# Recurrence of the next chunk between the feed-forward matmuls of this one, two heads on the partitions

## The chip, the cores and the metric

The kernel runs on one core of a Trainium2 chip. The metric is device time in microseconds; three runs of the kernel before took 493.35, 493.57 and 493.63 us, median 493.57.

## What is computed

A gated linear recurrence over 768 steps for each of 4 x 8 heads of size 48, and a bilinear feed-forward on its output (3072 tokens of 384 features, 1536 hidden). The kernel computes the recurrence in chunks of 128 steps with cumulative products of alpha; products of matrices are in bf16, the cumulative sum of logarithms in fp32.

```python
for t in range(S):
    state = alpha[:, :, t, :, None] * state + np.einsum('bhd,bhe->bhde', k[:, :, t], v[:, :, t])
    y[:, :, t] = np.einsum('bhd,bhde->bhe', q[:, :, t], state)
x = np.ascontiguousarray(y.transpose(0, 2, 1, 3)).reshape(B * S, H * D)
a = x @ w_a
b = x @ w_b
out = (a * b) @ w_out
```

## The kernel before, in words

The work has two stages, one after the other.

The first is the recurrence, a loop over six chunks of 128 steps (L65). SP loads alpha, q, k and v of the chunk for all 32 heads, 768 KB each (L68 to L74), into tiles with two buffers. ACT takes the logarithm (L81); PE forms cumulative sums with a triangular fp32 matrix, 512 columns at a time (L89); ACT makes the exponentials beta and invb (L90, L91); DVE makes Qp, Kp and Vb (L94 to L98). Then comes a loop over the 32 heads (L102), in which every tile has 48 partitions or 48 columns: PE transposes Qp and Kp (L105, L109), DVE copies both out of PSUM (L107, L111), PE forms the scores (L114), DVE masks them (L116), PE adds two products into y (L119, L120), DVE copies y (L121), PE forms the state update (L124) and the chunk's decay (L126), ACT and DVE write the new state (L128 to L131). All PSUM tiles of this stage have one buffer. At the chunk's end SP writes y, transposed, to xT in memory (L136).

The second stage is the feed-forward. When the pools of the first are closed (L138), POOL issues the loads of the weights (L146 to L150) and SP reads xT back (L155). Six tiles of 512 tokens follow (L162): for each of 12 hidden blocks three matmuls with wa (L168), which ACT copies (L170), three with wb (L173), and a product on DVE (L174); then for each of four groups of 128 tokens 12 matmuls with wo (L178), a copy on ACT (L180) and a store (L181).

The order of instructions on each engine is set by a scheduler, which moves them within what the buffers allow; the weights wait for the pools of the first stage.

## Time and profile before

| what | value |
|---|---|
| median of three runs | 493.57 us |
| span of the profiled execution | 492.8 us |
| PE busy | 441.8 us (90%) |
| DVE busy | 256.5 us (52%) |
| ACT busy | 190.8 us (39%) |
| POOL busy | 11.2 us (2%) |
| moved by DMA | 32.32 MB |

The profile is of one execution, whose recorded time is the span from its first to its last instruction; it is 0.8 us shorter than the median of the runs. Busy times are shares of this span. PE is TensorE, PEld its weight loads, DVE VectorE, ACT ScalarE, POOL GpSimd and SP the engine that issues most transfers. Matmuls overlap on PE, so their busy times add up to more than the work takes one after the other.

### The profile page before, as it was taken

To read this page: it belongs to the slowest core of one execution; us is meant where nothing else is said; L and a number is where in the kernel's file an instruction comes from. 1 tells how busy PE (TensorE), PEld (TensorE's weight loads), DVE (VectorE), ACT (ScalarE), POOL (GpSimd) and SP (SyncE) were. 2 spreads that over 40 slices of the span, in tenths; PEclk is the share of its full clock that TensorE was granted. 3 is DMA by queue.
4 is the path that set the end of the run, shared out by engine and by line. 5 is a ranking of instruction groups with operands and counts; after the bars stand their busy time and mean duration, and the time that the engine had idled before them with its cause. 6 is when DMAs were issued, how large, how long until landed. Compare 5 with 4: busy or idle time off the path is not lost.

```text
span 492.8 us, 7155 instructions
## 1 busy us (share of the span) xinstructions
PE 441.8 (90%) x2280; PEld 225.2 (46%) x2292; DVE 256.5 (52%) x1052; ACT 190.8 (39%) x534; POOL 11.2 (2%) x28
## 2 busy tenths in 40 slices
PE   2589989999899989998999799942899999999997
...
GB/s 163 187 97 137 73 138 73 136 110 59 139 112 9 10 128 81 9 10 1 10 8 18 8 7 12 11 86 264 137 17 48 34 32 41 25 49 16 65 0 66
DMA packets 114806, 32.32 MB, mean 66 GB/s; under 512 B 109008, under 2 KB 113616, under 8 KB 114768
## 3 DMA queue, kind: packets, MB, share of 16 engines
...
q14 instruction: 20, 0.16, 0.1%
...
## 4 chain that ended last, share of the span: by engine, by line
PE 85%; DMA 5%; ACT 5%; DVE 2%; issue 2%; POOL 1%; ACTq 0%; POOLq 0%; DVEq 0%
PE bp L173 10%; PE op L178 9%; PE ap L168 9%; PE bl_p L126 9%; PE yt_p L120 9%; PE qpt_p L105 8%; PE qk_p L114 8%; PE kpt_p L109 8%; PE cumlog L89 8%; PE yt_p L119 5%; DMA wb_t<-in_moe_w_b_dram 3%; PE kv_p L124 3%; ACT logA L81 2%; DMA a_tile<-in_alpha_dram 1%; ACT invb L91 1%
## 5 line engine op out<-in xcount | busy, mean ns | idle before, releaser
L131 ACT ACTIVATE S_all<-tmp,bl 48x48 bf16<-48x48 f32 x192 | 63.6, 333 | 149.9 <-PE yt_p L120 144.1
L174 DVE TENSOR_TENSOR prod<-a_sb,bp 128x512 bf16<-128x512 bf16 x72 | 49.5, 688 | 105.9 <-PE bp L173 105.6
L121 DVE CAST yT_all<-yt_p 48x128 bf16<-48x128 f32 x192 | 54.3, 283 | 85.7 <-PE yt_p L120 85.3
L168 PE MATMUL ap<-xt_sb,wa_t 128*128 128x512 bf16 x206 | 59.6, 393 | 15.4 <-DMA wa_t<-in_moe_w_a_dram 12.8
L170 ACT ACTIVATE a_sb<-ap 128x512 bf16<-128x512 f32 x72 | 43.0, 597 | 69.6 <-PE ap L168 65.6
L126 PE MATMUL bl_p<-ones_col,logA 128*48 128x1 f32 x384 | 61.3, 229 | 5.4 <-ACT bl L128 4.8
L116 DVE TENSOR_TENSOR masked<-qk_p,mask_bf 128x128 bf16<-128x128 f32 x192 | 55.9, 291 | 14.7 <-PE qk_p L114 6.5
L126 PEld LDWEIGHTS bl_p<-ones_col,logA 128*48 128x48 f32 x384 | 45.6, 175 | 38.5 <-issue 10.5
L173 PE MATMUL bp<-xt_sb,wb_t 128*128 128x512 bf16 x214 | 60.6, 389 | 2.8 <-DMA wb_t<-in_moe_w_b_dram 2.5
L109 PE MATMUL kpt_p<-ident,Kp 128*48 128x128 bf16 x192 | 57.8, 301 | 2.9 <-DVE Kp L96 2.9
L105 PE MATMUL qpt_p<-ident,Qp 128*48 128x128 bf16 x192 | 57.4, 299 | 0.5 <-DVE Qp L94 0.4
L120 PE MATMUL yt_p<-QpT,S_all 48*48 48x128 bf16 x192 | 57.4, 299 | 0.0
L119 PE MATMUL yt_p<-masked,Vb 128*48 128x128 bf16 x192 | 53.7, 280 | 3.0 <-DVE Vb L98 1.0
L114 PE MATMUL qk_p<-QpT,KpT 48*128 48x128 bf16 x192 | 54.5, 284 | 0.2 <-DVE KpT L111 0.2
L89 PE MATMUL cumlog<-logA,ut_f 128*128 128x512 f32 x36 | 37.3, 1140 | 16.5 <-ACT logA L81 12.7
L178 PE MATMUL op<-wo_t,prod 128*128 128x384 bf16 x288 | 47.8, 326 | 0.0
L124 PE MATMUL kv_p<-Vb,Kp 128*48 128x48 bf16 x192 | 41.9, 218 | 0.6 <-DVE Vb L98 0.6
L111 DVE COPY KpT<-kpt_p 48x128 bf16<-48x128 bf16 x192 | 39.6, 206 | 0.3 <-PE kpt_p L109 0.3
L168 PEld LDWEIGHTS <-wa_t 128*128 128x128 bf16 x216 | 21.5, 100 | 40.0 <-issue 13.8
L107 DVE COPY QpT<-qpt_p 48x128 bf16<-48x128 bf16 x192 | 39.6, 206 | 0.0
L130 DVE TENSOR_TENSOR tmp<-kv_p,S_all 48x48 f32<-48x48 f32 x192 | 36.6, 190 | 2.0 <-PE qpt_p L105 1.4
L178 PEld LDWEIGHTS <-prod 128*128 128x128 bf16 x288 | 28.2, 98 | 19.3
...
## 6 DMA issues: line engine op xcount, KB each, us to landing
a_tile<-in_alpha_dram SPq DMA_DIRECT2D x6, 768.0 KB, 8.4
q_tile<-in_q_dram SPq DMA_DIRECT2D x6, 768.0 KB, 9.5
k_tile<-in_k_dram SPq DMA_DIRECT2D x6, 768.0 KB, 7.3
v_tile<-in_v_dram SPq DMA_DIRECT2D x6, 768.0 KB, 8.6
...
xT<-yT_all SPq DMA_DIRECT2D x24, 96.0 KB, 2.1
xt_sb<-xT SPq DMA_DIRECT2D x3, 768.0 KB, 6.8
...
```

Source lines behind the costliest of these rows:

```text
L89: nc.tensor.matmul(p[:, : ssl.stop - ssl.start], lhsT=ut_f32, rhs=logA[:, ssl], start=True, stop=True)
L105: nc.tensor.transpose(qpt_p, Qp[:, hd], ident)
L109: nc.tensor.transpose(kpt_p, Kp[:, hd], ident)
L114: nc.tensor.matmul(qk_p, lhsT=KpT, rhs=QpT, start=True, stop=True)
L119: nc.tensor.matmul(yt_p, lhsT=Vb[:, hd], rhs=masked, start=True, stop=False)
L120: nc.tensor.matmul(yt_p, lhsT=S_all[:, bh, :], rhs=QpT, start=False, stop=True)
L124: nc.tensor.matmul(kv_p, lhsT=Kp[:, hd], rhs=Vb[:, hd], start=True, stop=True)
L126: nc.tensor.matmul(bl_p, lhsT=logA[:, hd], rhs=ones_col, start=True, stop=True)
L131: nc.scalar.activation(out=S_all[:, bh, :], in_=tmp, func=AF.Copy, scale=bl)
L168: nc.tensor.matmul(ap, lhsT=wa_t[:, kk, ff * 128:(ff + 1) * 128], rhs=xt_sb[:, kk, rsl], start=(kk == 0), stop=(kk == KTILES - 1))
L173: nc.tensor.matmul(bp, lhsT=wb_t[:, kk, ff * 128:(ff + 1) * 128], rhs=xt_sb[:, kk, rsl], start=(kk == 0), stop=(kk == KTILES - 1))
L178: nc.tensor.matmul(op, lhsT=prod[:, ff, m * 128:(m + 1) * 128], rhs=wo_t[:, ff, :], start=(ff == 0), stop=(ff == NFF - 1))
```

## The change

Both stages are merged. Two heads stand side by side on the partitions, each in 64 rows of which 48 are used (Qp and Kp are zero-padded to 64 columns a head, Sb holds the states of a pair on its diagonal). One transpose, one y accumulation with Sb and one state update serve a pair; scores and the masked products are made for each head in its half of the partitions or output rows. Work goes by batch (8 heads): stA is the cumulative sum and the exponentials, stB the products Kp and Qp, now on POOL, and the cast of v, stC the transposes and one copy, stD scores and masks, stY y, stK the state update. y is copied by ACT into xT in SBUF; the 16 spare rows of each half are filled with features of the fourth pair by six small transfers (fill). The weights' rows are permuted in their loads to fit. The decay is the last row of beta, written to memory and read back with the other layout (decay).

The order is now written out by hand (manual_schedule: each engine gets its instructions as they are written). Chunk 0's recurrence is done first, batch by batch; then for each chunk c the 12 hidden blocks ff_a, ff_b of the feed-forward, with steps of the recurrence of chunk c+1 in slots (the table todo) between ff_a and ff_b, and the loads of chunk c+2 issued at block 0; then four ff_o. All loads of chunks 0 and 1 come first on SP. POOL issues the loads of the weights in pieces among its products of chunk 0.

```diff
-    for c in range(NCHUNK):
...
-        for bh in range(BH):
...
-            nc.sync.dma_start(out=xT_r[:, b, :, sl], in_=yT_r[:, b, :, :])
...
-        nc.sync.dma_start(out=xt_sb[:, kk, :], in_=xT[kk * 128:(kk + 1) * 128, :])
...
+    ctx.enter_context(tc.manual_schedule())
+    cst = ctx.enter_context(tc.tile_pool(name="cst", bufs=1))
+    ld = ctx.enter_context(tc.tile_pool(name="ld", bufs=2))
+    wk = ctx.enter_context(tc.tile_pool(name="wk", bufs=2))
+    dram = ctx.enter_context(tc.tile_pool(name="dram", bufs=2, space=bass.MemoryType.DRAM))
+    ps = ctx.enter_context(tc.tile_pool(name="ps", bufs=1, space=bass.MemoryType.PSUM))
...
+    def load_ab(i):
+        fs = slice(i * WS, (i + 1) * WS)
+        for w, t in ((moe_w_a, wa_t), (moe_w_b, wb_t)):
+            two = w[:KT * 2 * D, fs].rearrange("(t r d) f -> r d t f", r=2, d=D)
+            rest = w[KT * 2 * D:, fs].rearrange("(r t g) f -> r g t f", r=2, g=G)
+            for r in range(2):
+                nc.gpsimd.dma_start(out=t[r * DP:r * DP + D, :, fs], in_=two[r])
+                nc.gpsimd.dma_start(out=t[r * DP + D:(r + 1) * DP, :, fs], in_=rest[r])
+    def load_o(i):
+        n = NFF // 4
+        nc.gpsimd.dma_start(out=wo_t[:, i * n:(i + 1) * n, :],
+                            in_=moe_w_out[i * n * 128:(i + 1) * n * 128, :].rearrange("(k p) f -> p k f", p=128))
...
+    def alloc_loads(ch):
+        ch.a = ld.tile([C, B, H, D], F32, name="a_t")
...
+    def load(ch, b):
+        if b == 0:
+            alloc_loads(ch)
+        sl = slice(ch.c * C, (ch.c + 1) * C)
+        for t, src in ((ch.a, alpha), (ch.k, k), (ch.q, q), (ch.v, v)):
+            nc.sync.dma_start(out=t[:, b], in_=src[b, :, sl, :].rearrange("h s d -> s h d"))
...
+    def stA(ch, b):
+        p = ps.tile([C, 512], F32, name="t2")[:, :H * D]
+        nc.tensor.matmul(p, lhsT=ut_f32, rhs=ch.la[:, b], start=True, stop=True)
+        nc.scalar.activation(out=ch.beta[:, b], in_=p, func=AF.Exp)
+        nc.scalar.activation(out=ch.invb[:, b], in_=p, func=AF.Exp, scale=-1.0)
+    def stB(ch, b):
+        i = ch.c % 2
+        nc.gpsimd.tensor_mul(Kp[i][:, b, :, :D], ch.k[:, b], ch.invb[:, b].rearrange("p (h d) -> p h d", h=H))
+        nc.gpsimd.tensor_mul(Qp[i][:, b, :, :D], ch.q[:, b], ch.beta[:, b].rearrange("p (h d) -> p h d", h=H))
+        nc.vector.tensor_copy(ch.vb[:, b], ch.v[:, b])
+    def decay(ch):
+        if ch.c == NCH - 1:
+            return
+        row = dram.tile([1, B * P2, 2, D], F32, name="row")
+        nc.sync.dma_start(out=row.rearrange("o a r d -> o (a r d)"), in_=ch.beta[C - 1:C].rearrange("o b f -> o (b f)"))
+        for r in range(2):
+            nc.sync.dma_start(out=ch.bl[r * DP:r * DP + D].rearrange("d b a -> d (b a)"),
+                              in_=row[:, :, r, :].rearrange("o a d -> d (o a)"), allow_slow_non_contiguous=True)
+    def stC(ch, b):
+        i = ch.c % 2
+        t = ps.tile([C, 2, P2, C], BF16, name="t1")
+        for p in range(P2):
+            for j, src in enumerate((Qp[i], Kp[i])):
+                nc.tensor.transpose(t[:, j, p, :], src[:, b, 2 * p:2 * p + 2, :].rearrange("s h d -> s (h d)"), ident)
+        ch.qk = wk.tile([C, 2, P2, C], BF16, name="qk", bufs=3)
+        nc.vector.tensor_copy(ch.qk.rearrange("p j a s -> p (j a s)"), t.rearrange("p j a s -> p (j a s)"))
+    def stD(ch, b):
+        se = ps.tile([C, P2, C], F32, name="se")
+        so = ps.tile([C, P2, C], F32, name="so")
+        for p in range(P2):
+            nc.tensor.matmul(se[:, p, :], lhsT=ch.qk[0:DP, 1, p, :], rhs=ch.qk[0:DP, 0, p, :], start=True, stop=True)
+            nc.tensor.matmul(so[:, p, :], lhsT=ch.qk[DP:2 * DP, 1, p, :], rhs=ch.qk[DP:2 * DP, 0, p, :], start=True, stop=True)
+        ch.me = wk.tile([C, P2, C], BF16, name="me")
+        ch.mo = wk.tile([C, P2, C], BF16, name="mo")
+        nc.vector.tensor_mul(ch.me, se, mask4)
+        nc.vector.tensor_mul(ch.mo, so, mask4)
+        ch.qkD = ch.qk
+    def stY(ch, b):
+        y = ps.tile([C, P2, C], F32, name="t2")
+        for p in range(P2):
+            nc.tensor.matmul(y[:, p, :], lhsT=Sb[:, b, p, :], rhs=ch.qkD[:, 0, p, :], start=True, stop=False, skip_group_check=True)
+            nc.tensor.matmul(y[0:D, p, :], lhsT=ch.vb[:, b, 2 * p, :], rhs=ch.me[:, p, :], start=False, stop=True, skip_group_check=True)
+            nc.tensor.matmul(y[DP:DP + D, p, :], lhsT=ch.vb[:, b, 2 * p + 1, :], rhs=ch.mo[:, p, :], start=False, stop=True, skip_group_check=True)
+        nc.scalar.activation(out=ch.xT[:, :, b, :], in_=y[:, :KT, :], func=AF.Copy)
+        nc.scalar.activation(out=ch.y3[:, b, :], in_=y[:, KT, :], func=AF.Copy)
+    def fill(ch):
+        for r in range(2):
+            for t in range(KT):
+                nc.sync.dma_start(out=ch.xT[r * DP + D:(r + 1) * DP, t], in_=ch.y3[r * DP + t * G:r * DP + (t + 1) * G])
+    def stK(ch, b):
+        if ch.c == NCH - 1:
+            return
+        i = ch.c % 2
+        kv = ps.tile([C, 512], F32, name="t1")[:, :P2 * 2 * D].rearrange("p (a e) -> p a e", a=P2)
+        for p in range(P2):
+            nc.tensor.matmul(kv[:, p, :], lhsT=Kp[i][:, b, 2 * p:2 * p + 2, :].rearrange("s h d -> s (h d)"),
+                             rhs=ch.vb[:, b, 2 * p:2 * p + 2, :].rearrange("s h d -> s (h d)"), start=True, stop=True)
+        tmp = wk.tile([C, P2, D], F32, name="tmp")
+        for r in range(2):
+            rs = slice(r * DP, r * DP + D)
+            nc.vector.tensor_add(tmp[rs], kv[rs, :, r * D:(r + 1) * D], Sb[rs, b, :, r * DP:r * DP + D])
+            nc.gpsimd.tensor_mul(Sb[rs, b, :, r * DP:r * DP + D], tmp[rs],
+                                 ch.bl[rs, b, :].rearrange("p (a o) -> p a o", o=1).broadcast_to([D, P2, D]))
+    def ff_a(ch, f):
+        if f == 0:
+            ch.prod = wk.tile([128, NFF, NT], BF16, name="prod")
+        x = ch.xT.rearrange("p k b s -> p k (b s)")
+        ap = ps.tile([128, NT], F32, name="f", bufs=4)
+        for kk in range(KT):
+            nc.tensor.matmul(ap, lhsT=wa_t[:, kk, f * 128:(f + 1) * 128], rhs=x[:, kk, :], start=(kk == 0), stop=(kk == KT - 1))
+        ch.as_ = wk.tile([128, NT], BF16, name="as_", bufs=3)
+        nc.scalar.activation(out=ch.as_, in_=ap, func=AF.Copy)
+    def ff_b(ch, f):
+        x = ch.xT.rearrange("p k b s -> p k (b s)")
+        bp = ps.tile([128, NT], F32, name="f", bufs=4)
+        for kk in range(KT):
+            nc.tensor.matmul(bp, lhsT=wb_t[:, kk, f * 128:(f + 1) * 128], rhs=x[:, kk, :], start=(kk == 0), stop=(kk == KT - 1))
+        nc.vector.tensor_mul(ch.prod[:, f, :], ch.as_, bp)
+    def ff_o(ch, m):
+        op = ps.tile([128, NT], F32, name="f", bufs=4)[:, :d_model]
+        for f in range(NFF):
+            nc.tensor.matmul(op, lhsT=ch.prod[:, f, m * C:(m + 1) * C], rhs=wo_t[:, f, :], start=(f == 0), stop=(f == NFF - 1))
+        ot = wk.tile([128, d_model], F32, name="ot", bufs=3)
+        nc.scalar.activation(out=ot, in_=op, func=AF.Copy)
+        nc.sync.dma_start(out=out[m * S + ch.c * C:m * S + (ch.c + 1) * C, :], in_=ot)
+    for b in range(B):
+        load(chunks[0], b)
+    for b in range(B):
+        load(chunks[1], b)
+    c0 = chunks[0]
+    for b in range(B):
+        logs(c0, b)
+        stA(c0, b)
+        stB(c0, b)
+        if b == B - 1:
+            decay(c0)
+        if b == 1:
+            load_ab(0)
+        if b == 2:
+            load_ab(1)
+        stC(c0, b)
+        stD(c0, b)
+        stY(c0, b)
+    fill(c0)
+    for b in range(B):
+        stK(c0, b)
+    load_ab(2)
+    load_ab(3)
+    for i in range(4):
+        load_o(i)
+    logs(chunks[1])
+    stA(chunks[1], 0)
+    stB(chunks[1], 0)
+    stA(chunks[1], 1)
+    stB(chunks[1], 1)
+    for c in range(NCH):
+        ch = chunks[c]
+        nx = chunks[c + 1] if c + 1 < NCH else None
+        n2 = chunks[c + 2] if c + 2 < NCH else None
+        todo = {}
+        if nx is not None:
+            todo = {
+                0: lambda: stA(nx, 2), 1: lambda: stB(nx, 2), 2: lambda: (stC(nx, 0), stA(nx, 3)),
+                3: lambda: (stD(nx, 0), stB(nx, 3), decay(nx)), 4: lambda: stC(nx, 1), 5: lambda: (stY(nx, 0), stK(nx, 0), stD(nx, 1)),
+                6: lambda: stC(nx, 2), 7: lambda: (stY(nx, 1), stK(nx, 1), stD(nx, 2)), 8: lambda: stC(nx, 3),
+                9: lambda: (stY(nx, 2), stK(nx, 2), stD(nx, 3)), 11: lambda: (stY(nx, 3), fill(nx), stK(nx, 3)),
+            }
+        for f in range(NFF):
+            ff_a(ch, f)
+            if n2 is not None and f == 0:
+                for b in range(B):
+                    load(n2, b)
+            if n2 is not None and f == NFF - 1:
+                logs(n2)
+            if f in todo:
+                todo[f]()
+            ff_b(ch, f)
+        for m in range(B):
+            ff_o(ch, m)
+            if n2 is not None and m >= 2:
+                stA(n2, m - 2)
+                stB(n2, m - 2)
```

On PE, in the recurrence of before, one head of the loop stands in a row (names: yt_p is y, qpt_p and kpt_p are transposes, qk_p scores, bl_p decay, kv_p the state update):

```order
L119 LDWEIGHTS Vb
L119 MATMUL yt_p<-masked,Vb 48x128
L120 LDWEIGHTS S_all
L120 MATMUL yt_p<-QpT,S_all 48x128
L105 LDWEIGHTS Qp
L105 MATMUL qpt_p<-ident,Qp 48x128
L114 LDWEIGHTS KpT
L114 MATMUL qk_p<-QpT,KpT 128x128
L109 LDWEIGHTS Kp
L109 MATMUL kpt_p<-ident,Kp 48x128
L126 MATMUL bl_p<-ones_col,logA 48x1
```

On PE after the change, at slot 5 of chunk 0, the last of three matmuls of ff_a (f is the feed-forward's PSUM tile) is followed by the first pair of stY (t_582 is y; me and mo are the masked scores of the even and the odd head):

```order
L205 MATMUL f<-xT,wa_t 128x512
L171 LDWEIGHTS Sb
L171 MATMUL t_582<-qk,Sb 128x128
L172 LDWEIGHTS vb
L172 MATMUL t_582<-me,vb 48x128
L173 LDWEIGHTS vb
L173 MATMUL t_582<-mo,vb 48x128
```

The y matmuls, which stood among those of other steps of a head, now stand pair by pair between two groups of feed-forward matmuls.

On DVE, in the recurrence of before, one head reads:

```order
L121 CAST yT_all<-yt_p 48x128
L130 TENSOR_TENSOR tmp<-kv_p,S_all 48x48
L116 TENSOR_TENSOR masked<-qk_p,mask_bf 128x128
L107 COPY QpT<-qpt_p 48x128
L111 COPY KpT<-kpt_p 48x128
```

On DVE after the change, at slots 5 and 6 of chunk 0 (prod is the feed-forward's product, tmp the state sum, qk the copied transposes):

```order
L214 TENSOR_TENSOR prod<-as__558,f 128x512
L194 TENSOR_TENSOR tmp<-t_597,Sb 48x192 x2
L164 TENSOR_TENSOR me<-se,mask 128x512
L165 TENSOR_TENSOR mo<-so,mask 128x512
L214 TENSOR_TENSOR prod<-as__580,f 128x512
L154 COPY qk<-t_632 128x1024
```

Steps of the recurrence now stand, in larger tiles, between the feed-forward's products.

On POOL, which before only issued the weights' loads, the last weight loads now stand ahead of the products of chunk 1:

```order
L80 DMA wb_t<-in_moe_w_b_dram 48x3x384
L81 DMA wb_t<-in_moe_w_b_dram 16x3x384
L85 DMA wo_t<-in_moe_w_out_dram 128x3x384 x4
L133 TENSOR_TENSOR Kp_94<-k_t,invb 128x8x48
L134 TENSOR_TENSOR Qp_92<-q_t,beta 128x8x48
```

The products moved from DVE to POOL, behind the transfers that POOL issues.

## Rows read from the trace of the kernel before

**Rows 1.** Page, busy time by engine: us (share of the span) x instructions

```profile
PE 441.8 (90%) x2280; PEld 225.2 (46%) x2292; DVE 256.5 (52%) x1052; ACT 190.8 (39%) x534; POOL 11.2 (2%) x28
```

**Rows 2.** Stages: start:end length, busy of each engine (instructions), clock, DMA share, GB/s

```profile
67.50:119.28 51.78, 49.52 (x264) 25.72 (x263) 34.26 (x164) 22.69 (x74) 0.00 (x0) 1.00 0.69 102
326.70:349.57 22.87, 5.57 (x12) 1.31 (x14) 0.56 (x1) 0.87 (x3) 8.04 (x15) 1.00 0.95 229
349.57:353.40 3.83, 3.83 (x10) 1.36 (x9) 1.35 (x3) 1.01 (x2) 1.62 (x4) 1.00 1.27 190
353.68:489.15 135.47, 134.88 (x688) 68.17 (x697) 47.45 (x69) 52.48 (x92) 0.00 (x0) 1.00 0.10 34
489.15:492.80 3.65, 0.00 (x0) 0.00 (x0) 0.00 (x0) 0.49 (x1) 0.00 (x0) 1.00 0.16 57
```

**Rows 3.** Chain that ended last, in order of time: start us, us, what

```profile
8.55 2.06 PE cumlog L89 x2
...
349.77 1.71 PE ap L168 x4
...
354.28 0.65 PE ap L168 x3
...
364.64 7.80 PE op L178 x48
...
387.98 7.80 PE op L178 x48
```

**Rows 4.** Timeline, recurrence, PE: start us, us, engine line operation, idle before

```profile
24.30 0.30 PE L109 MATMUL kpt_p<-ident,Kp 128*48 128x128 bf16 x1
...
24.39 0.31 PE L105 MATMUL qpt_p<-ident,Qp 128*48 128x128 bf16 x1
...
100.86 0.30 PE L120 MATMUL yt_p<-QpT,S_all 48*48 48x128 bf16 x1
...
101.09 0.30 PE L105 MATMUL qpt_p<-ident,Qp 128*48 128x128 bf16 x1
...
101.19 0.28 DVE L121 CAST yT_all<-yt_p 48x128 bf16<-48x128 f32 x1 [0.36 <-PE yt_p L120]
```

**Rows 5.** Groups by line and shape: xcount | busy us, mean ns | idle before, releasers

```profile
L174 DVE TENSOR_TENSOR prod<-a_sb,bp 128x512 bf16<-128x512 bf16 x72 | 49.5, 688 | 105.9 <-PE bp L173 105.6 <-ACT a_sb L170 0.3
L170 ACT ACTIVATE a_sb<-ap 128x512 bf16<-128x512 f32 x72 | 43.0, 597 | 69.6 <-PE ap L168 65.6 <-PE bp L173 3.5
L107 DVE COPY QpT<-qpt_p 48x128 bf16<-48x128 bf16 x192 | 39.6, 206 | 0.0
L130 DVE TENSOR_TENSOR tmp<-kv_p,S_all 48x48 f32<-48x48 f32 x192 | 36.6, 190 | 2.0 <-PE qpt_p L105 1.4 <-ACT bl L128 0.2
L180 ACT ACTIVATE sb<-op 128x384 f32<-128x384 f32 x24 | 11.8, 491 | 38.6 <-PE op L178 38.6
L96 DVE TENSOR_TENSOR Kp<-k_tile,invb 128x1536 bf16<-128x1536 f32 x6 | 10.5, 1742 | 0.0
L81 ACT ACTIVATE logA<-a_tile 128x1536 f32<-128x1536 f32 x6 | 8.9, 1483 | 5.0 <-DMA a_tile<-in_alpha_dram 4.9
L81 ACT ACT_TABLE_LOAD x6 | 7.7, 1283 | 0.8 <-PEq L196 0.7
L98 DVE CAST Vb<-v_tile 128x1536 bf16<-128x1536 f32 x6 | 5.7, 949 | 0.0
```

**Rows 6.** POOL: a group by line, then its timeline at the weights' loads

```profile
masks.py:66 POOL TENSOR_SCALAR_AFFINE_SELECT ut_f<-ut_f 128x128 f32<-128x128 f32 x1 | 0.3, 283 | 0.0
...
332.64 1.12 POOL L150 DMA_DIRECT2D wo_t<-in_moe_w_out_dram  x2
338.55 0.53 POOL L150 DMA_DIRECT2D wo_t<-in_moe_w_out_dram  x1 [4.79 <-DMA wa_t<-in_moe_w_a_dram]
```

**Rows 7.** Page, DMA issues: out<-in xcount, KB each, median us to landing; and GB/s by slices

```profile
GB/s 163 187 97 137 73 138 73 136 110 59 139 112 9 10 128 81 9 10 1 10 8 18 8 7 12 11 86 264 137 17 48 34 32 41 25 49 16 65 0 66
...
a_tile<-in_alpha_dram SPq DMA_DIRECT2D x6, 768.0 KB, 8.4
xT<-yT_all SPq DMA_DIRECT2D x24, 96.0 KB, 2.1
```

More of the change, by code (lines that the diff above doesn't have):

```diff
@@ L12 @@
 AF = mybir.ActivationFunctionType
+ALU = mybir.AluOpType
 @with_exitstack
@@ L50 @@
     make_upper_triangular(nc, ut_f32, val=1.0, diag=True)
-    mask_bf = cst.tile([C, C], BF16, name="mask_bf")
-    make_upper_triangular(nc, mask_bf, val=1.0, diag=True)
-    ones_col = cst.tile([C, 1], F32, name="ones_col")
-    nc.vector.memset(ones_col, 1.0)
-    S_all = cst.tile([D, BH, D], BF16, name="S_all")
-    nc.vector.memset(S_all, 0.0)
-    gla = ExitStack()
-    chpool = gla.enter_context(tc.tile_pool(name="chunk", bufs=2))
-    hpool = gla.enter_context(tc.tile_pool(name="head", bufs=4))
@@ L138 @@
-    gla.close()
-    wpool = ctx.enter_context(tc.tile_pool(name="wpool", bufs=1))
-    KTILES = d_model // 128
-    NFF = d_ff // 128
-    wa_t = wpool.tile([128, KTILES, d_ff], BF16, name="wa_t")
-    wb_t = wpool.tile([128, KTILES, d_ff], BF16, name="wb_t")
-    for kk in range(KTILES):
-        nc.gpsimd.dma_start(out=wa_t[:, kk, :], in_=moe_w_a[kk * 128:(kk + 1) * 128, :])
-        nc.gpsimd.dma_start(out=wb_t[:, kk, :], in_=moe_w_b[kk * 128:(kk + 1) * 128, :])
-    wo_t = wpool.tile([128, NFF, d_model], BF16, name="wo_t")
@@ new lines @@
+    mask = cst.tile([C, C], BF16, name="mask")
+    make_upper_triangular(nc, mask, val=1.0, diag=True)
+    mask4 = mask.rearrange("p (o s) -> p o s", o=1).broadcast_to([C, P2, C])
+    Sb = cst.tile([C, B, P2, 2 * DP], BF16, name="Sb")
+    nc.vector.memset(Sb, 0.0)
+    Qp, Kp = [], []
+    for i in range(2):
+        t = cst.tile([C, B, H, DP], BF16, name=f"Qp{i}")
+        nc.vector.memset(t, 0.0)
+        Qp.append(t)
+        t = cst.tile([C, B, H, DP], BF16, name=f"Kp{i}")
+        nc.vector.memset(t, 0.0)
+        Kp.append(t)
@@ new lines, in load_o @@
+    def load_o(i):
+        n = NFF // 4
+        nc.gpsimd.dma_start(out=wo_t[:, i * n:(i + 1) * n, :],
+                            in_=moe_w_out[i * n * 128:(i + 1) * n * 128, :].rearrange("(k p) f -> p k f", p=128))
+    class Chunk:
+        pass
+    chunks = []
+    for c in range(NCH):
+        ch = Chunk()
+        ch.c = c
+        chunks.append(ch)
+    def alloc_loads(ch):
+        ch.a = ld.tile([C, B, H, D], F32, name="a_t")
+        ch.k = ld.tile([C, B, H, D], F32, name="k_t")
+        ch.q = ld.tile([C, B, H, D], F32, name="q_t")
+        ch.v = ld.tile([C, B, H, D], F32, name="v_t")
@@ new lines @@
+    logs(chunks[1])
[3 more added lines that the diff above has]
+    stB(chunks[1], 1)
+    for c in range(NCH):
+        ch = chunks[c]
[24 more added lines that the diff above has]
+                stB(n2, m - 2)
```

124 lines of the change are left out of this document (24 added, 100 removed).

## The prediction

> **What bounds the kernel now.** I read the page's busy shares first: PE is busy for 90% of the span, DVE for 52%, POOL for 2% [rows 1]. A busy PE alone says little, since its matmuls overlap, so I cut the span into stages [rows 2]. One chunk of the recurrence lasts 51.78 us with PE busy for 49.52 of it; six chunks fill the first 327 us. Then 22.87 us pass in which PE works for 5.57 us: x goes to memory and back and the weights arrive. The six feed-forward tiles take the last 139 us, and 3.65 us pass after the last matmul.
>
> The chain of waits shows what one feed-forward tile costs [rows 3]: its 48 output matmuls take 7.80 us, and those of the next tile begin 387.98 - 364.64 = 23.34 us later. It also shows the clock. Three 512-column matmuls take 0.65 us from 354.28 us on (0.216 us each, 512 columns at 2.4 GHz), but four take 1.71 us at 349.77 us (0.427 each, 512 at 1.2 GHz). The granted clock is printed as 1.00 for both stretches [rows 2]; the spacing decides, and by it PE ran at the lower level when the dense feed-forward began and rose within its first tile. For the recurrence the timeline agrees [rows 4]: two 128-column matmuls of one shape start 24.39 - 24.30 = 0.09 us apart, near 128 columns at 1.2 GHz (0.107), and pairs of different shapes 0.23 us apart (100.86 to 101.09). So the recurrence is a stream of small matmuls at the lower level, each paying about twice its columns. The feed-forward is at its columns already.
>
> **What the change does, part by part.** I write the new time as P + 5K + F + ends: a prologue P up to the first feed-forward matmul, five chunks K in which feed-forward c and recurrence c+1 share PE, one feed-forward tile F alone.
>
> *Removed:* the 22.87 us hand-over through memory, and the 192 x 8 small matmuls of the per-head loop (two of the eight are L126's one-column fp32 passes).
>
> *K, PE.* Feed-forward per chunk is what it was: 23.3 us at the upper level. Recurrence per batch is 8 transposes, 8 scores, 12 for y, 4 for the state: 32 matmuls, 128 per chunk for 32 heads. No 128-column matmul at the upper level is in the trace. Lower bound: the 384-column matmuls, 7.80/48 = 0.1625 us, a third of which is 0.054; upper bound: the 0.23 us of mixed shapes. Of the two I build a value: every matmul pays 0.054, and each change of shape the difference of the two rows at the lower level, 0.23 - 0.09 = 0.14. The changes per batch are two for each of the four pairs in y (full width, then 48 columns) and two around the scores, ten in all: 32 x 0.054 + 10 x 0.14 = 3.1 us, four times 12.5, nearer the lower bound, since most neighbours now have one shape. Bounds for the 128: 6.9 and 29.4. The cumulative sum is fp32: 2.06 us for 512 columns at the lower level [rows 3], so 1.55 for 384; at the upper level between half (0.8) and all of it; I take 1.0, four of them 4.0 us, bounds 3.2 and 6.2. PE together: 23.3 + 12.5 + 4.0 = 39.8.
>
> *K, the others* [rows 5], per chunk. DVE: 12 prod x 0.69, 8 masks x 0.69 (the same shape), 4 copies of 1024 (between 0.67 and 1.13 from the 0.206 of 128, I take 1.13), 8 state sums x 0.34, 4 casts x 0.3 = 22.2 us. ACT: 12 x 0.60, 12 x 0.49 (outputs and x), 8 exps x 0.49, 4 x 0.27, a log of 1.48 and two table loads of 1.28 = 20.2. POOL below 12. None reaches 39, so PE bounds the chunk if each slot's answer is back before the next slot. Between two slots lie one ff_b and one ff_a, 1.3 us, plus the slot's own matmuls; the longest answer, copy 1.13 behind a prod of 0.69, needs 1.8. I cost the handovers at 3 us a chunk, bounds 0 and 6. That cover is gone if DVE has a backlog. **K = 43**, bounds 33.4 and 65.
>
> One wait is new: the decay goes through memory (row, then two reads), queued on SP behind 16 loads of chunk c+2. Four loads of 768 KB, 8.4 us each to landing but overlapping, moved at some 170 GB/s, take about 18 us; add two transfers of 2.1 us [rows 7] and two lots of 768 four-byte pieces: the decay lands some 25 us after the chunk's start. The state product on POOL waits for it, and DVE's third state sum (slot 9, some 24 us in) waits for POOL because tmp has two buffers; behind it stand masks and prod. That is the handover I expect to see, 0 to 3 us, inside the 3 us above.
>
> *P.* It is a serial chain at the lower clock, four passes, one per batch, since each engine's order is fixed; durations are scaled from [rows 3 to 5]: log 0.49, sum 1.6, two exps 0.87, K and Q products on POOL, 8 transposes 1.06 (0.107 each and 0.2 to end), copy 1.13, scores 1.3 (8 x 0.16), masks 1.38, y 1.8 (the ten matmuls behind the masks, 0.16 each and 0.2), evictions 0.76, table load 1.28, and 0.6 for hand-overs. POOL has never multiplied here; its affine select of 128 columns took 0.283 us [rows 6], so 384 cost 0.85; the DVE product row (1.74 for 1536) would give 0.44. I take POOL's own row, 1.7 for two. Sum 14.0, four times 56, plus 3.5 until the first slice of alpha lands (between the 2.1 and the 8.4 us of [rows 7]), less one table load: 58. Then the four state updates and two cumulative sums of chunk 1, 9 us. **P = 67**, bounds 54 and 78. The casts of v on DVE run at the same time, and no row of before shows both engines at work on SBUF. The Trainium skill (SBUF — State Buffer, Who interferes with whom) says that DVE in a two-port copy or cast and GpSimd exclude each other for a whole instruction, which speaks against products on POOL; by it each product could wait for one cast of about 0.3 us, 1.2 us in the four passes, and the sum would be 316.
>
> *Chunk 0* pays extra, S. POOL issues 16 + 4 weight transfers before the products of chunk 1; an issue takes 0.55 us, and the ninth waited 4.79 us for the first to land [rows 6]. So the products come about 11 to 16 us after the state update, while slot 2 asks for them 8 us after the first matmul: a stall near 5 us, and some matmuls before and after it at the lower level, 4 us. **S = 9**, bounds 0 and 20. The last recurrence chunk has no state update and two sums less: -3. The ends are F = 23.3 and 3.7.
>
> Sum: 67 + 5 x 43 + 9 - 3 + 27 = **315 us**, against the 492.8 us span of the profiled execution; the median of the runs, 493.57, is 0.8 longer, which is nothing at this size. 0.2%, or 1 us, is about what a measurement of this kernel can tell from no change. With all bounds together it would be 245 or 447; terms that err independently give 280 to 350.
>
> **Rivals.** *Clock falls in the slots.* The rows that speak for it: the recurrence matmuls kept PE at the lower level for 327 us although PE was 90% busy. If the slots do so again and only ff_o runs fast, with 0.17 a small matmul (halfway between 0.107 and 0.23), a chunk is 72 x 0.427 + 7.8 + 128 x 0.17 + 2 x 1.6 + 2 x 1.0 = 65.5, and the time, with S = 0, 418. Against: dense feed-forward stands between all slots, and it raised the clock within one tile. *Handovers show.* If each of 11 slots waits 1.5 us for DVE (a copy and a hand-over) in place of 3 us in all, K = 56.5 and the time 382; for it speaks that DVE waited 0.36 us for PE in every head of before [rows 4], against it the 1.8 us reckoned above. *Heads run side by side.* Scores and masked products of a pair use different halves of the partitions or of the output rows. If they overlap on PE, the price falls to the lower bound 0.054 and, with no waits, K to 33.4, P to 60, S to 4, and the time is 255; no row speaks for it, since all heads of before use the same partitions, and against it stand the 0.23 us between neighbours of different rows [rows 4]. The Trainium skill (TensorE: Matmul & The Clock Gate, Part 3: Packing small matmuls) says that matmuls on different row or column groups run concurrently, about 4 ns apart; no run here shows it yet, and it is this rival. *Slower.* The clock stays low in the feed-forward as well, because slots interrupt it, and small matmuls cost what mixed shapes cost now, 0.23: F = 72 x 0.427 + 48 x 0.325 = 46.3, K = 46.3 + 29.4 + 4 x 1.6 = 82, P = 78, S = 0, the time 535. At 0.17 and P = 67 it would be 486; from 0.18 us a matmul on, with the clock always low, the change loses. There the change moves work under a matmul stream that became twice as long, so it would not do what it says.
>
> **How the numbers follow.** Forecast 0.52 (280 to 350), clock in the slots 0.17, handovers 0.16, side by side 0.10, slower or even 0.05. The range 275 to 410 holds the forecast, the handovers and the better half of the clock rival, 8 in 10. All but the last case are far faster: faster 0.95, within 0.2% 0.01, slower 0.04.
>
> **What would show it.** Right: ff_b and ff_a of three matmuls 0.65 us apart between slots; a chunk period of 38 to 48 us between two ff_o; 60 to 75 us before the first feed-forward matmul; POOL's products of chunk 1 late in slot 2. Wrong: 512-column matmuls 0.43 us apart in the slots of chunks 1 to 4 (clock); PE idle before me, mo or the copied qk in most slots (handovers); transposes or scores 0.2 us apart (price of a matmul); a period over 50 us.

## The result and the profile after

The changed kernel takes 281.94 us (median of four runs, 280.39 to 282.33) against 493.6 us: a ratio of 0.5705, 95% interval 0.5689 to 0.572. That is inside the predicted range and 2 us above the lower end of the forecast's own range (280 to 350); the value of 315 was 33 us too high. The profiled execution has a span of 280.6 us, 1.3 us below the median.

The page's busy times after the change (us, share of the span, instructions), to be read beside [rows 1]:

```profile
PE 231.5 (82%) x1520; PEld 120.6 (43%) x1520; DVE 120.3 (43%) x213; ACT 122.8 (44%) x219; POOL 89.7 (32%) x134
```

DVE has a fifth of its instructions left and less than half of its time; POOL now multiplies. The stages answer to [rows 2] (start:end length, busy of PE, PEld, DVE, ACT, POOL with counts, granted clock, DMA share, GB/s). They are cut at the first feed-forward matmul of each chunk; chunks 2 and 3 repeat chunk 1:

```profile
0.00:60.83 60.83, 26.37 (x141) 12.72 (x141) 17.48 (x31) 23.40 (x33) 24.75 (x46) 1.00 0.75 133
60.83:109.56 48.73, 40.01 (x258) 20.58 (x257) 19.17 (x36) 19.07 (x35) 22.22 (x34) 0.89 0.70 119
109.56:146.24 36.68, 36.03 (x257) 19.25 (x256) 19.60 (x36) 18.97 (x35) 11.84 (x17) 1.00 0.53 111
...
219.62:253.41 33.79, 33.48 (x238) 17.84 (x237) 16.62 (x26) 13.78 (x29) 7.17 (x8) 1.00 0.07 26
253.41:276.60 23.19, 23.19 (x121) 11.65 (x119) 8.24 (x12) 9.12 (x16) 0.00 (x0) 1.00 0.09 32
276.60:280.55 3.95, 0.31 (x2) 0.00 (x0) 0.00 (x0) 0.49 (x1) 0.00 (x0) 1.00 0.20 76
```

The 1.00 printed for the prologue is not what PE ran at: the clock record begins at 63.4 us only, and in the prologue the transposes of batch 1 start 0.107 us apart (six steps from 21.84 to 22.48 us), which is 128 columns at the lower level. From chunk 1 on PE is busy for 36.0 of 36.7 us, so it bounds the chunk, as predicted; DVE and ACT have half of it, POOL a third. Put into the prediction's sum:

| term | predicted | measured | difference in the sum |
|---|---|---|---|
| P, up to the first feed-forward matmul | 67 | 60.8 | -6.2 |
| K, one chunk, five times | 43 | 36.7 | -31.5 |
| S, extra of chunk 0 (48.73 - 36.69) | 9 | 12.0 | +3.0 |
| last recurrence chunk (33.79 - 36.69) | -3 | -2.9 | +0.1 |
| F and end | 27 | 27.1 | +0.1 |
| sum | 315 | 280.6 | -34.5 |

Inside a chunk, PE's timeline shows what a slot costs (start us, duration us, engine, line, operation; durations overlap, so spacings are read). It answers to [rows 4]; slots 6 and 7 of chunk 1:

```profile
127.49 0.81 PE L205 MATMUL f<-xT,wa_t 128*128 128x512 bf16 x3
128.14 0.22 PE L152 MATMUL t<-ident,Qp 128*128 128x128 bf16 x1
128.19 0.22 PE L152 MATMUL t<-ident,Kp 128*128 128x128 bf16 x1
...
129.23 0.81 PE L205 MATMUL f<-xT,wa_t 128*128 128x512 bf16 x3
129.88 0.22 PE L171 MATMUL t<-qk,Sb 128*128 128x128 bf16 x1
130.03 0.24 PE L172 MATMUL t<-me,vb 128*48 128x128 bf16 x1
130.03 0.24 PE L173 MATMUL t<-mo,vb 128*48 128x128 bf16 x1
130.20 0.23 PE L171 MATMUL t<-qk,Sb 128*128 128x128 bf16 x1
...
131.19 0.34 PE L189 MATMUL t<-vb,Kp 128*128 128x96 bf16 x4
131.47 0.23 PE L160 MATMUL se<-qk 64*128 64x128 bf16 x1
131.47 0.23 PE L161 MATMUL so<-qk 64*128 64x128 bf16 x1
```

Three 512-column matmuls take 0.65 us (127.49 to 128.14), 0.216 each: the upper level, in the slots too. Transposes stand 0.055 us apart, the lower bound of the prediction. The two scores of a pair begin at the same printed time, and so do the two masked products of a pair: they run side by side. A pair of y takes 0.33 us (129.88 to 130.20).

The stall of chunk 0, on PE and POOL:

```profile
65.36 0.81 PE L205 MATMUL f<-xT,wa_t 128*128 128x512 bf16 x3
74.55 0.29 PE L152 MATMUL t<-ident,Qp 128*128 128x128 bf16 x1 [8.38 <-POOL Qp L134]
...
70.94 1.54 POOL L85 DMA_DIRECT2D wo_t<-in_moe_w_out_dram  x2 [0.20 <-issue]
72.56 0.98 POOL L133 TENSOR_TENSOR Kp<-k_t,invb 128x384 bf16<-128x384 f32 x1
73.51 0.98 POOL L134 TENSOR_TENSOR Qp<-q_t,beta 128x384 bf16<-128x384 f32 x1
```

Slot 2 waited 8.38 us for POOL's products, which stood behind 20 issues of weight transfers (58.58 to 72.5 us), the place that the prediction named. The profiler's clock record is at the lower level from 70.2 to 80.4 us and at the upper one from there to the end: the 512-column matmuls that begin at 76.77 us are 0.43 us apart, those at 80.86 us 0.216. The first three of the chunk, from 60.83 us on, were 0.43 us apart as well.

One pass of the prologue (batch 1), all engines:

```profile
16.55 0.52 ACT L123 ACTIVATE la<-a_t 128x384 f32<-128x384 f32 x1
...
21.75 0.29 PE L152 MATMUL t<-ident,Qp 128*128 128x128 bf16 x1 [2.98 <-POOL Qp L134]
...
22.83 0.69 DVE L154 COPY qk<-t 128x1024 bf16<-128x1024 bf16 x1 [9.71 <-PE t L152]
...
23.58 0.29 PE L160 MATMUL se<-qk 64*128 64x128 bf16 x1 [0.79 <-DVE qk L154]
...
24.22 0.69 DVE L164 TENSOR_TENSOR me<-se,mask 128x512 bf16<-128x512 f32 x1 [0.70 <-PE se L160]
...
29.20 0.52 ACT L123 ACTIVATE la<-a_t 128x384 f32<-128x384 f32 x1
```

It takes 12.65 us (16.55 to 29.20) where 14.0 were reckoned: the copy 0.69 us in place of 1.13, the eight scores 0.64 (23.58 to 24.22) in place of 1.3. POOL's product takes 0.99 us in the mean. In the groups by line, the state sum reads (mean ns after the comma, then idle time before and its releasers):

```profile
L194 DVE TENSOR_TENSOR tmp<-t,Sb 48x192 f32<-48x192 f32 x40 | 14.2, 355 | 24.3 <-PE t L189 20.3 <-POOL Sb L195 3.4
```

DVE waited for POOL's state product, and so for the decay, for 3.4 us in the whole run: the new wait is there and small.

### The profile page after: what moved, and what is told of

Its sections match the earlier page's. It is cut to its first block, busy times and chain, and to the rows that moved or that the text cites. A ratio compares the mean times of both kernels' runs of the same rounds, so it can differ in the third digit from the quotient of the medians.

```text
span 280.6 us, 4180 instructions
## 1 busy us (share of the span) xinstructions
PE 231.5 (82%) x1520; PEld 120.6 (43%) x1520; DVE 120.3 (43%) x213; ACT 122.8 (44%) x219; POOL 89.7 (32%) x134
## 4 chain that ended last, share of the span: by engine, by line
PE 76%; POOL 6%; issue 6%; ACT 4%; DMA 3%; DVE 3%; POOLq 0%; DVEq 0%; ACTq 0%
PE f L213 17%; PE f L219 17%; PE f L205 15%; PE t L127 7%; PE t L172 6%; PE t L171 5%; PE t L152 5%; PE se L160 3%; PE t L189 2%; DMA wa_t<-in_moe_w_a_dram 2%; POOL Kp L133 2%; ACT invb L129 2%; POOL Qp L134 2%; DMA a_t<-in_alpha_dram 1%; POOL wo_t L85 1%
## 5 line engine op out<-in xcount | busy, mean ns | idle before, releaser
L205 PE MATMUL f<-xT,wa_t 128*128 128x512 bf16 x216 | 59.7, 386 | 0.0
L213 PE MATMUL f<-xT,wb_t 128*128 128x512 bf16 x216 | 59.5, 385 | 0.0
L219 PE MATMUL f<-wo_t,prod 128*128 128x384 bf16 x288 | 48.4, 326 | 0.0
L133 POOL TENSOR_TENSOR Kp<-k_t,invb 128x384 bf16<-128x384 f32 x24 | 23.8, 992 | 65.6 <-ACT invb L129 65.5
L195 POOL TENSOR_TENSOR Sb<-tmp,bl 48x192 bf16<-48x192 f32 x40 | 20.1, 502 | 70.6 <-DMA bl<-row 43.4
L127 PE MATMUL t<-la,ut_f 128*128 128x384 f32 x48 | 26.9, 649 | 15.8 <-ACT la L123 12.2
L219 PEld LDWEIGHTS <-prod 128*128 128x128 bf16 x288 | 28.2, 98 | 20.2 <-issue 0.9
L172 PE MATMUL t<-me,vb 128*48 128x128 bf16 x96 | 23.6, 246 | 2.3 <-DVE me L164 2.3
L173 PE MATMUL t<-mo,vb 128*48 128x128 bf16 x96 | 23.6, 246 | 1.3 <-DVE mo L165 1.3
L134 POOL TENSOR_TENSOR Qp<-q_t,beta 128x384 bf16<-128x384 f32 x24 | 24.3, 1012 | 0.0
L171 PE MATMUL t<-qk,Sb 128*128 128x128 bf16 x96 | 22.8, 237 | 0.0
```

The source lines that it names most:

```text
L127: nc.tensor.matmul(p, lhsT=ut_f32, rhs=ch.la[:, b], start=True, stop=True)
L133: nc.gpsimd.tensor_mul(Kp[i][:, b, :, :D], ch.k[:, b], ch.invb[:, b].rearrange("p (h d) -> p h d", h=H))
L134: nc.gpsimd.tensor_mul(Qp[i][:, b, :, :D], ch.q[:, b], ch.beta[:, b].rearrange("p (h d) -> p h d", h=H))
L171: nc.tensor.matmul(y[:, p, :], lhsT=Sb[:, b, p, :], rhs=ch.qkD[:, 0, p, :], start=True, stop=False, skip_group_check=True)
L172: nc.tensor.matmul(y[0:D, p, :], lhsT=ch.vb[:, b, 2 * p, :], rhs=ch.me[:, p, :], start=False, stop=True, skip_group_check=True)
L173: nc.tensor.matmul(y[DP:DP + D, p, :], lhsT=ch.vb[:, b, 2 * p + 1, :], rhs=ch.mo[:, p, :], start=False, stop=True, skip_group_check=True)
```

## Experiments

Theory, after the two traces: the change is worth what it is because small matmuls between dense ones run at the upper clock level, and of the 33 us that were missed about half is the price of small matmuls. Rivals: packing does it and the slots don't matter; heads side by side, not the clock, make small matmuls cheap; the cost of POOL or of the weights' order is somewhere else than it seems.

**The steps of the slots in one block** after the 12 hidden blocks of the feed-forward.

```diff
-            if f in todo:
-                todo[f]()
             ff_b(ch, f)
+        for f in sorted(todo):
+            todo[f]()
```

> All steps of the recurrence of chunk c+1 stand in one block between the 12 hidden blocks and the output matmuls of chunk c; nothing else differs. Theory (the slots hide the chain's waits and keep the clock at the upper level): the block shows copy, masks and evictions one after another and its matmuls fall to the lower level, some 22 to 25 us in place of the 11 us that PE needs for it in the slots; the chunk period goes from 36.7 to 46 to 50 us and the time to 330 to 345 us. Rival (packing two heads made the gain, the slots little): the period stays within 2 us of 36.7 and the time within 282 to 292 us.

Measured: 336.34 us, ratio 0.6813 (0.6799 to 0.6827); chunks 1 to 3 take 48.7 to 50.5 us. Two neighbouring stretches, cut at changes of the clock record (columns as in the stages above); the first lies in chunk 0, the second holds mostly the feed-forward of chunk 1:

```profile
83.70:111.00 27.30, 20.36 (x136) 11.08 (x137) 11.09 (x22) 8.39 (x16) 8.04 (x12) 0.50 0.11 17
111.00:138.30 27.30, 23.70 (x122) 11.88 (x120) 9.22 (x14) 15.24 (x25) 3.91 (x4) 1.00 0.67 146
```

The clock falls in the block of steps, where PE waits for other engines, and comes back in the feed-forward, in each of chunks 0 to 4. So the gain has two parts. The recurrence of before and its feed-forward tile cost 51.78 + 23.3 = 75.1 us a chunk [rows 2, 3]; the feed-forward and the packed steps in a block, 48.9 (the middle one of the three); in slots, 36.7. The slots are worth 12 us a chunk, in two parts of about the same size: in chunk 1 of the block run PE is busy for 42.06 us in place of 36.03, at a mean granted clock of 0.82, and idle for 6.6 in place of 0.7. The other 26 us go to packing together with what else changed in a chunk (products on POOL, larger tiles on DVE, y kept in SBUF); no run takes these apart.

**The weights' loads spread over the prologue's passes,** one piece a pass, wo behind the first two pairs of products of chunk 1.

```diff
-        if b == 1:
-            load_ab(0)
-        if b == 2:
-            load_ab(1)
+        load_ab(b)
...
-    load_ab(2)
-    load_ab(3)
-    for i in range(4):
-        load_o(i)
     logs(chunks[1])
...
     stB(chunks[1], 1)
+    for i in range(4):
+        load_o(i)
```

> The four pieces of the weights wa and wb are issued one in each pass of the prologue, and wo only after the first two products of chunk 1. Theory (PE's 8.4 us in slot 2 of chunk 0 are POOL's queue of 20 transfers ahead of the products, and the fall of the clock follows from that stop): the wait goes, the clock does not fall, and 8.4 + 2.6 us for the matmuls that ran at half rate go with it: 271 us (268 to 274). Rival (weights or loads are late themselves): the wait moves to a transfer and the time stays within 3 us of 282.

Measured: 271.56 us, ratio 0.5498 (0.549 to 0.5506). Chunk 0 now reads:

```profile
60.80:98.77 37.97, 37.63 (x258) 19.74 (x256) 19.15 (x36) 19.09 (x35) 14.19 (x20) 1.00 0.66 120
```

48.73 became 37.97 us at a granted clock of 1.00: the stall and the low stretch behind it were POOL's issues. Chunk 0 gained 10.8 us and the run 10.4. The 1.3 us by which chunk 0 is still longer than the others fit its first matmuls, which are at the lower level (three of 512 columns take 1.29 us from 60.80 us on, although the row prints 1.00).

**The y matmuls with Sb first, then the four pairs.** Two runs. The first keeps the start flag on each of the four Sb matmuls; its y lacks the state's term for three of the four pairs. The second sets the flag for the first only (the diff shows this flag and the new order).

```diff
         for p in range(P2):
-            nc.tensor.matmul(y[:, p, :], lhsT=Sb[:, b, p, :], rhs=ch.qkD[:, 0, p, :], start=True, stop=False, skip_group_check=True)
+            nc.tensor.matmul(y[:, p, :], lhsT=Sb[:, b, p, :], rhs=ch.qkD[:, 0, p, :], start=(p == 0), stop=False, skip_group_check=True)
+        for p in range(P2):
```

> In y the four full-width matmuls with the state come first and then the four pairs of 48 columns: two changes of shape per batch in place of eight. Theory (a change of shape costs about 0.1 us at the upper level, beside 0.055 for a matmul of the same shape): 1.32 us per batch become about 0.7, 12 us less over the 20 batches in slots and some 4 us less in the four passes of the prologue, 266 us (263 to 270). Rival (each matmul that adds to a region waits for the one before it on that region, or the 48-column matmuls cost that much by themselves): no change, within 2 us of 282.

> As the run with y in groups, but only the first of the four full-width matmuls has the start flag, since a start clears the marks of its whole PSUM bank. The instructions and their order are the same, so by the theory of shape changes the time is that run's, 264 us (262 to 266), with the whole of y computed. Rival (that run was fast because accumulations were dropped): 275 to 282 us.

Measured: 264.3 us, ratio 0.5353 (0.5344 to 0.5362), and 264.27 us, 0.5344 (0.5326 to 0.5362). A chunk takes 34.04 us in both, 2.65 less. PE's timeline of the second:

```profile
123.62 0.39 PE L171 MATMUL t<-qk,Sb 128*128 128x128 bf16 x4
123.93 0.24 PE L173 MATMUL t<-me,vb 128*48 128x128 bf16 x1
123.94 0.24 PE L174 MATMUL t<-mo,vb 128*48 128x128 bf16 x1
124.01 0.22 PE L173 MATMUL t<-me,vb 128*48 128x128 bf16 x1
```

The second pair of masked products starts 0.08 us after the first, the later ones 0.05 to 0.06 apart; y costs 0.66 us a batch less. Of the eight changes of shape two are left, so one change cost about 0.66/6 = 0.11 us, where 0.14 was reckoned from [rows 4]. The order within one accumulation was worth 17.6 us. The gain by itself leaves a rival, that a matmul waits for the one before it on its own output, which the new order also sets apart. The starts speak against it. The first masked product stands 0.15 us behind the last Sb matmul (123.93, where the four Sb matmuls begin 0.055 us apart from 123.62) although its own output was written three matmuls earlier; in the changed kernel it stands as far, 0.15 us, behind its own (129.88 to 130.03), and the next Sb matmul, on another output, 0.17 us behind it (130.20).

**The products Kp and Qp on DVE,** `nc.vector.tensor_mul` for `nc.gpsimd.tensor_mul` in stB.

> The products Kp and Qp are made by DVE in place of POOL. Theory (DVE takes 0.55 us for one, POOL 0.98; DVE has 17 us to spare in a chunk of 36.7): the four passes of the prologue get 0.9 us shorter each, the products of chunk 1 no longer stand behind the transfers, so that the 8.4 us wait and its 2.6 us at the lower level go, and the chunk period stays at 36.7: 267 us (264 to 271). Rival (DVE's fixed order puts products ahead of masks and prod): up to 8 x 0.55 = 4.4 us more in each of four chunks, and the time 275 to 286 us.

Measured: 274.61 us, ratio 0.5558 (0.5547 to 0.5569), between the two. The rival's price for DVE's order did not come, since chunks 1 to 3 did not grow. A product takes 0.55 us on DVE against 0.99 on POOL; P fell to 56.9 us and chunks 1 to 3 to 36.51. Chunk 0 took 45.9 us, 2.8 less than in the changed kernel and 7.9 more than with the weights spread. Its waits (engine and line that waited, on whom: us in total, times, longest):

```profile
POOL Sb L195 <- DMA bl<-row: 16.8, 1, 16.8
...
DVE tmp L194 <- POOL Sb L195: 7.6, 1, 7.6
...
PE t L172 <- DVE me L164: 5.1, 1, 5.1
```

With POOL's products out of the way, chunk 0 ran into the wait that the prediction had named: the decay, then DVE's state sum, the masks behind it, and PE.

**The scores not in pairs,** four of the even heads and then four of the odd ones.

> The four score matmuls of the even heads come first and then the four of the odd heads, in place of one by one. Theory (neighbours in different halves of the partitions run side by side, which is one reason why a batch costs PE 2.4 us and not the forecast 3.1): the eight take 0.44 us in place of 0.24 at the upper level and 0.86 in place of 0.44 at the lower, 0.2 us x 20 batches and some 0.3 x 4: 287 us (284 to 290). Rival (the weight loads or the shape set the pace, not the halves): no change, within 1.5 us of 282.

Measured: 281.55 us, ratio 0.5695 (0.5682 to 0.5707): no change. But the trace does not show the order that was written:

```profile
120.67 0.23 PE L160 MATMUL se<-qk 64*128 64x128 bf16 x1
120.68 0.23 PE L162 MATMUL so<-qk 64*128 64x128 bf16 x1
120.73 0.22 PE L160 MATMUL se<-qk 64*128 64x128 bf16 x1
120.75 0.22 PE L162 MATMUL so<-qk 64*128 64x128 bf16 x1
```

The odd heads' scores (L162) start 0.01 to 0.02 us behind the even heads', though three others stand between them in the program. The period agrees: chunks 1 to 3 take 36.72 to 36.73 us against 36.69. Had the eight started in the written order, with only the fourth and fifth side by side, they would have taken seven spacings of 0.055 us in place of four, 0.66 us a chunk more (an estimate). So the edit did not take the side-by-side work away, and the run tells nothing about its worth. The next one was made for that.

**The odd heads' scores from the even heads' half of the partitions.** The work keeps its amount, but the odd heads get the even heads' scores: their own are left out.

```diff
-            nc.tensor.matmul(so[:, p, :], lhsT=ch.qk[DP:2 * DP, 1, p, :], rhs=ch.qk[DP:2 * DP, 0, p, :], start=True, stop=True)
+            nc.tensor.matmul(so[:, p, :], lhsT=ch.qk[0:DP, 1, p, :], rhs=ch.qk[0:DP, 0, p, :], start=True, stop=True)
```

> The odd heads' score products read the even heads' half of the partitions (rows 0:64) as well, so that the two heads of a pair cannot run beside each other in the array; the odd heads' scores are thereby those of the even heads, and the rest of the work is the same. Theory: the pair's two score products run side by side in the changed kernel (0.01 us apart), and this is worth one product (about 0.05 us) for each of 4 pairs in 20 batches, 4 us, and some 0.4 us in each of the 4 prologue chunks: 285 to 290 us, with the spacing of the scores of a pair 0.05 us or more. Rival: products of different halves cost no less than products of one half, and the time stays at 281 to 283 us.

Measured: 287.0 us, ratio 0.5816 (0.5797 to 0.5834), 5.1 us more than the changed kernel. A chunk takes 37.57 us, 0.88 more, which is 0.055 for each of its 16 pairs:

```profile
122.83 0.23 PE L160 MATMUL se<-qk 64*128 64x128 bf16 x1
122.89 0.22 PE L161 MATMUL so<-qk 64*128 64x128 bf16 x1
```

The scores now stand 0.06 us apart. Side by side is real and saves one matmul of two; for the scores it is worth 5 us of 282.

**A prologue in which the passes overlap:** all of alpha's loads and logarithms first, transposes of batch b+1 before y of batch b, chunk 1's loads behind the decay, and the weights in pieces, as in the run that spreads them. Run without and with the grouped y.

```diff
+    for b in range(B):
+        logs(c0, b)
+    stA(c0, 0)
+    stB(c0, 0)
...
+    for b in range(B):
+        if b + 1 < B:
+            stC(c0, b + 1)
+        stY(c0, b)
+        if b == B - 1:
+            fill(c0)
+        stK(c0, b)
+        if b + 1 < B:
+            stD(c0, b + 1)
+            load_ab(b + 1)
```

> The prologue is written as the slots are: the alphas load first, four logs, then the steps of the four batches overlapped, the weights in pieces behind the batches' last products, the loads of chunk 1 after the decay. Theory (P is a serial chain of 12.65 us a batch, of which no engine works more than 5 us): P falls from 60.8 to 40 us (36 to 46), and with POOL's queue out of slot 2 the time is 250 us (246 to 258). Rival (the prologue is bound by loads and the lower clock): P stays over 52 us, and only the 11 us of the weights' order are won, 268 to 272 us.

> The overlapped prologue and y in groups with one start flag together. Theory (PE's own matmuls set the chunk period, so that both gains add): 250 - 14 = 236 us (230 to 245), chunk period 34.0 us. Rival (with PE shorter, DVE or the loads become the bound of the chunk): period 36 us or more, 244 to 252 us.

Measured: 265.01 us, ratio 0.5373 (0.5349 to 0.5396), and 252.48 us, 0.5103 (0.5079 to 0.5127). P came down to 52.6 and 52.5 only, so that beyond the weights' order (271.56) the rest is worth 6.5 us. The first row is PE's wait in the run without the grouped y, the second SP's timeline:

```profile
PE f L206 <- DMA xT<-y: 13.0, 1, 13.0
...
44.95 3.82 SPq L182 DMA_DIRECT2D xT<-y  x6
```

PE was done with chunk 0's recurrence before 40 us and then waited 13.0 us for the six fill transfers, which SP issued at 44.95 us behind the 16 loads of chunk 1. Neither theory had this wait; the first rival's P (over 52 us) came through the order on SP's queue. With the grouped y, chunks 2 and 3 take 34.0 to 34.1 us, so the second rival, another bound of the chunk, did not come, and the 236 us expected were missed mostly in the prologue.

**Where chunk 1's loads stand.** Three runs on top of the last kernel (overlapped prologue, grouped y): the loads of k, q and v behind the fill; half of them ahead of it; and that half with, in chunk 0, the loads of chunk 2 behind the decay (the diff is of the third).

```diff
         if b == B - 1:
             fill(c0)
+            for j in range(2, B):
+                load(chunks[1], j, (1, 2, 3))
...
-            if n2 is not None and f == 0:
+            if n2 is not None and f == 0 and c > 0:
...
             if f in todo:
                 todo[f]()
+            if f == 3 and c == 0:
+                for j in ((0,), (1, 2, 3)):
+                    for b in range(B):
+                        load(n2, b, j)
```

> The kernel with the overlapped prologue and the grouped state products, with the 16 loads of chunk 1 issued behind the transfers that fill chunk 0's x, and not ahead of them. Theory: the prologue's end was set by those transfers, which stood behind the loads on SP's queue; now the first feed-forward matmul comes at 38 to 46 us instead of 52.5, and the whole takes 236 to 246 us. Rival: the wait moves to slot 2 of chunk 0, whose products of k and q now have their loads later, or to the feed-forward weights, and the time stays at 248 us or above.

> As the kernel with the fill transfers ahead of chunk 1's loads, but only half of the loads of k, q and v (batches 2 and 3) behind those transfers and the half of batches 0 and 1 ahead. Theory: each of the two kernels before it lost on one side what it won on the other (PE waited 16.5 us for the fill with all loads ahead, and chunk 0 took 57.7 us with all behind); with the half that slots 1 to 3 need ahead, the first feed-forward matmul comes at 40 to 47 us, chunk 0 takes 37 to 43 us, and the time is 241 to 249 us. Rival: the 32 loads of chunks 0 and 1 and those of the weights take a fixed time on the queues whatever their order, so chunk 1's first feed-forward matmul comes no earlier than 90 us and the time stays at 252 to 256 us.

> As the kernel with the split loads, and in chunk 0 the 16 loads of chunk 2 are issued behind the decay of chunk 1 and not ahead of it. Theory: the decay then lands before slot 9 and the state sums of chunk 0 do not wait for it, which is worth 2 to 5 us over the split loads alone: 238 to 246 us; chunk 1 stays at 34.0 us, since the logarithms of chunk 2 come only in block 11. Rival: chunk 0 is bound by the loads of k and q and not by the decay, or the later loads of chunk 2 hold up its logarithms at block 11: no gain over the split loads, or up to 5 us more.

Measured: 256.01 us, ratio 0.5178 (0.5143 to 0.5214); 254.07 us, 0.5139 (0.5118 to 0.5161); 240.47 us, 0.4872 (0.4854 to 0.4889). The first two start the feed-forward early (36.0 and 41.7 us) and lose it again in chunk 0 (57.7 and 50.2 us), so both expectations of a gain from the order of the loads fell. In the first, 7.2 us of PE's waits in chunk 0 are for products and copies whose loads now came later, as its rival said, and 6.6 us for the masks. The waits in the run with the split loads, on PE, DVE and POOL, then the issues of the decay's row on SP in this run and in the third, say on what:

```profile
PE t L174 <- DVE me L165: 11.5, 2, 11.0
...
DVE tmp L196 <- POOL Sb L197: 15.3, 2, 13.1
...
POOL Sb L197 <- DMA bl<-row: 20.8, 2, 20.5
...
70.11 0.38 SPq L143 DMA_DIRECT2D row<-beta  x1
...
49.33 0.25 SPq L143 DMA_DIRECT2D row<-beta  x1
```

It is the decay again: its row was issued at 70.11 us, behind 16 loads of chunk 2. In the third run it was issued at 49.33 us, DVE waited 2.3 us for POOL in place of 15.3, and prologue and chunk 0 read:

```profile
0.00:41.19 41.19, 21.93 (x141) 12.25 (x142) 18.28 (x31) 16.57 (x29) 30.63 (x56) 1.00 1.02 176
41.19:77.05 35.86, 35.52 (x257) 19.03 (x256) 19.98 (x36) 17.81 (x33) 17.12 (x24) 1.00 0.98 178
```

Chunk 0 became 14.3 us shorter by this one edit (which also puts alpha's loads ahead of the other twelve). The rival of the split loads, a fixed time of all loads whatever their order, had the right time (254.07 in 252 to 256, chunk 1 from 91.8 us on) for the wrong reason: the same loads in the third order let chunk 1 begin at 77.05 us. 240.47 us is the best time of the study, 41.5 us below the changed kernel and within what was expected of it.

## Why the prediction was right, and where it was off

**What bounds the chunk: right.** PE bounds it, at the upper level, with DVE, ACT and POOL under it. The rivals of a low clock in the slots (418) and of handovers that show (382) did not come: the spacing in the slots is 0.216 us for 512 columns, and PE waits 0.7 us in chunk 1. DVE has 19.6 us where 22.2 were reckoned, ACT 19.0 where 20.2 were (that sum comes out with 8 x 0.49, four outputs and four x, and not with the 12 that stand in it). The block run shows that the first of them was close: with the same steps out of the slots the clock falls in every chunk.

**K, 43 reckoned, 36.7 measured: the step that was mis-sized.** Of the 6.3 us half is the price of small matmuls. P erred the same way and S the other way by 3 us, so no large errors cancelled. Feed-forward 23.3 was right. The 32 matmuls of a batch take 2.4 us (transposes 0.45, y 1.3, state 0.27, scores 0.33) where 3.1 were reckoned, 3 us a chunk. Its formula charged every matmul 0.054 and ten changes of shape 0.14. Runs showed that the two scores of a pair share one slot of 0.055 (the run with one half, 0.22 us a batch), that a change costs about 0.11 (the grouped y, some 0.3 for ten), and the trace that the masked products of a pair also start together (about 0.2; no run undid this). The cumulative sums take 0.70 to 0.75 us, not 1.0 (another 1 us a chunk). What is left for handovers is 36.7 - 23.3 - 9.4 - 2.9 = 1.1 us in place of 3.

**Side by side, the rival at 255: half of it came.** Pairs do overlap, against the forecast. The Trainium skill (TensorE: Matmul & The Clock Gate, Part 3: Packing small matmuls) says that matmuls on different row or column groups of the array run concurrently, and the trace agrees, with starts 0.01 us apart or less. But the rival also dropped the price of a change of shape, and this stayed, at 0.11 us. The Trainium skill (TensorEngine Tiling (Array Packing), Key Properties) says that changing the tiling mode drains TensorE. The 2.65 us a chunk that the grouped y gave back agree with a cost at each change.

**P, 67 reckoned, 60.8 measured.** Four passes of 12.65 us in place of 14.0 (copy, scores) ended 4.8 us earlier, and state updates and cumulative sums of chunk 1 took 7.6 us in place of 9. POOL's product was nearer its own row of before [rows 6] (0.99 us against 0.85) than DVE's (0.44). The copy of 1024 columns was scaled from the 0.206 us of a copy of 128 [rows 5]; it took 0.69, its lower bound and as long as a mask of 512.

**S, 9 reckoned, 12.0 measured.** The place and the cause were right, and the run with the spread weights shows it. The stall was 8.38 us, not 5, since slot 2 asked 5.3 us after the first matmul (66.2 us) and not 8; the low stretch cost 12.0 - 8.4 = 3.6 us, as reckoned (4).

**The decay** held DVE up for 3.4 us in all, and in chunk 1 none of PE's 0.7 us is for it, where 0 to 3 us a chunk were allowed. It is nothing while something else is late: runs that removed other waits of chunk 0 met it, with DVE waiting 7.6 us (products on DVE), 8.7 (fill first) and 13.1 (split loads), and issuing its transfers ahead of chunk 2's loads gave 13.6 us of the time.

**POOL beside DVE: right at nothing on the path, though not for want of the effect.** DVE's cast of v takes 0.35 us alone and 0.97 beside a product:

```profile
112.72 0.99 POOL L133 TENSOR_TENSOR Kp<-k_t,invb 128x384 bf16<-128x384 f32 x1
112.95 0.97 DVE L135 CAST vb<-v_t 128x384 bf16<-128x384 f32 x1
113.67 1.11 POOL L134 TENSOR_TENSOR Qp<-q_t,beta 128x384 bf16<-128x384 f32 x1
...
118.20 0.35 DVE L135 CAST vb<-v_t 128x384 bf16<-128x384 f32 x1
```

The cast ends 0.2 us after the product does, so that most of its 0.35 us seems to lie behind the product, and the next product is 0.12 us longer. The Trainium skill (SBUF — State Buffer, Who interferes with whom) says that a DVE cast in a two-port mode and a GpSimd instruction exclude each other for the whole instruction. The trace is near that; full exclusion would put the cast's end 0.35 us behind the product. In the prologue pass shown no cast met a product. DVE is busy for 20 of 36.7 us, and PE waits for it in no row of chunk 1, so it cost nothing here.
